# Operations of the first eighteen head pairs issued in another order

## The chip, the cores and the metric

The kernel runs on one core of a Trainium2 chip. The core has TensorE (PE: matmuls, with weight loads shown apart as PEld), VectorE (DVE), ScalarE (ACT), GpSimd (POOL), and SyncE (SP), which here only issues DMAs. Each engine works through its own queue strictly in the order in which the program gave it the instructions; engines wait for one another through semaphores. The metric is the device time of one execution in microseconds (us), median over runs.

## The reference

Two operators in a row, float32 in and out. Cosine attention over 8 batches, 12 heads, 448 positions and a head width of 64, then a feed-forward block with the activation h * relu6(h + 3) / 6 on the 3584 x 768 result.

```
q_n = q / (norm(q) + 1e-6);  k_n = k / (norm(k) + 1e-6)
scores = q_n @ k_n.T / tau            # tau = 0.1
attn = softmax(scores)                # 448 x 448 for each batch and head
x = (attn @ v), heads side by side    # 3584 x 768
h = x @ w_in                          # 768 x 2048
out = (h * clip(h + 3, 0, 6) / 6) @ w_out   # 2048 x 768
```

## The kernel before

The heads of a batch are taken two at a time, so there are 48 pairs, six to a batch. One load brings the queries, or the keys, of two pairs: an item (448 KB); items 2d and 2d+1 hold the queries and keys of pairs 2d and 2d+1 (up to item 13; from 14 on keys come first). An item is loaded (LQ), squared (SQ), summed along the head width (RE), made into a reciprocal norm (NO: logarithm and exponent on ACT, the last two of four steps on DVE where the name ends in v), scaled and cast to bf16 (NM), and transposed on PE into a PSUM bank (TR; from item 14 on by a DMA, XD). Copies CQ, CK and CS take the transposed queries and keys out of the bank. LV and VC load and cast the values.

For a pair, SC makes the scores in four groups (0 to 3; group 3 holds the last 64 keys of both heads), EX is the exponential on ACT, VA multiplies by the values on PE, FI divides by the row sums on DVE, and BK and CX (or the DMAs XP and XB) bring the result, transposed, into the block's input `xT`. A number behind the name is the item or pair, then the group; a letter is the engine: a for ACT, v for DVE, p for POOL. SQ.5.a.4.3 is the square of item 5 on ACT, three of its seven parts from part 4.

The block's first matmul takes units U of six matmuls each (one 128-wide slice of the 2048, all 448 rows of one batch); UA (relu on ACT) and UV (product on DVE) empty its PSUM bank. A batch's units need all six of its pairs, so the first U needs CX.0 to CX.5. The weights come by twelve DMAs W that POOL issues in its own queue: the first eight bring `w_in` in quarters of two DMAs (U 1 to 4 of a batch need the first two, 5 to 8 the next two, 9 to 12 the next, 13 to 16 the last), the other four `w_out`. W casts from float32 to bf16 on the way. From the 31st U on a unit is one of sixteen matmuls of the second product.

DP.n puts n filler matmuls on zeros into PE's queue (`busy_pv`, line 935 before and 934 after; D.n is line 930), which have no reader and no result that is used.

The order of the first eighteen pairs is written out in `PLAN`, a list of such operations in program order; the lines of `PLAN` are run one after the other by `run`, and each operation appends its instructions to the queues of its engines. So an operation that stands earlier in `PLAN` stands earlier in each of its queues, and nothing else orders them but data and buffers. In the first six pairs the scores go to two double banks in turn (the last figure of SC.i.g.bank); after `OPEN` six single banks are used in a ring, in the order of program. Seven float32 buffers hold items, so item 8 can be loaded once item 1 is scaled, and so on. After `PLAN` a loop does pairs 18 to 47 in a fixed pattern that the change does not touch.

```
def load_qk(j, *heads):
    needs(("NM", raw_before(j)))
...
def mm1_unit(b, fc):
    needs(*(("CX", i) for i in range(b * HP, (b + 1) * HP)))
    assert len(weights) <= 10 - 2 * (4 * fc // FCN)
...
def next_weights():
    o, w = weights.pop(0)
    nc.gpsimd.dma_start(out=o, in_=w)
...
    for line in PLAN:
        run(line)
```

Of the kernel before, what the change touches and what calls it, by code (L numbers as in the profile page):

```python
# [1110 lines left out]
```

## Time and profile before

| | before |
|---|---|
| median of 3 runs | 406.54 us (403.97, 406.54, 407.21) |
| profiled execution | span 404.4 us, 9618 instructions; the page gives no time of that execution outside its span |
| busy, share of the span | PE 393.7 us (97%), DVE 288.7 (71%), ACT 276.7 (68%), POOL 236.7 (59%) |
| granted TensorE clock | 1.00 over the whole span |
| DMA | 63.75 MB, mean 158 GB/s |

The busy share of PE counts the filler matmuls as work, and counts overlapping matmuls once. In the views below, a row of the timeline reads: start, length of the (merged) row, engine, line, operation, tiles, how many, and in brackets the idle time of the engine before it with what ended it. A row of the windows reads: from, to, length, then the busy time and count of each engine, the granted clock, the DMA share and GB/s.

### The profile page before, as it was taken

To read this page: it belongs to the slowest core of one execution; us is meant where nothing else is said; L and a number is where in the kernel's file an instruction comes from. 1 tells how busy PE (TensorE), PEld (TensorE's weight loads), DVE (VectorE), ACT (ScalarE), POOL (GpSimd) and SP (SyncE) were. 2 spreads that over 40 slices of the span, in tenths; PEclk is the share of its full clock that TensorE was granted. 3 is DMA by queue.
4 is the path that set the end of the run, shared out by engine and by line. 5 is a ranking of instruction groups with operands and counts; after the bars stand their busy time and mean duration, and the time that the engine had idled before them with its cause. 6 is when DMAs were issued, how large, how long until landed. Compare 5 with 4: busy or idle time off the path is not lost.

```text
span 404.4 us, 9618 instructions
## 1 busy us (share of the span) xinstructions
PE 393.7 (97%) x3689; PEld 234.5 (58%) x3689; DVE 288.7 (71%) x512; ACT 276.7 (68%) x604; POOL 236.7 (59%) x232
## 2 busy tenths in 40 slices
PE   7798999999999999999999999999999999999996
PEld 5566656555665555655555556555565556555564
DVE  5898787878498777777857887587656666655663
ACT  4899989887377687687768768768758755225230
POOL 4799945862744997588486875876664600510070
PEclk9999999999999999999999999999999999999999
DMA  8899999999877748786779659986863523140134
GB/s 285 247 235 243 221 221 213 170 219 202 181 168 179 167 111 209 185 222 129 169 200 194 140 149 163 180 190 136 193 147 76 112 45 63 36 88 20 25 74 99
DMA packets 93166, 63.75 MB, mean 158 GB/s; under 512 B 56128, under 2 KB 93120, under 8 KB 93120
## 3 DMA queue, kind: packets, MB, share of 16 engines
q1 hardware_dynamic: 87408, 56.45, 61.1%
q0 software_dynamic: 5312, 6.29, 9.5%
q8 instruction: 29, 0.48, 0.6%
q10 hardware_dynamic: 400, 0.39, 0.3%
q14 instruction: 17, 0.14, 0.1%
HBM read 45.61 MB, written 11.01 MB: 140 GB/s over the span
## 4 chain that ended last, share of the span: by engine, by line
PE 88%; ACT 4%; DVE 3%; DMA 3%; SPq 1%; issue 0%; DVEq 0%; ACTq 0%
PE M L580 23%; PE M L753 16%; PE PV L475 11%; PE Y L580 6%; PE Z L580 6%; PE M L435 6%; PE Z L753 5%; PE Y L753 4%; PE M L833 3%; PE M L627 3%; ACT at L453 3%; DMA big<-in_q_dram 3%; PE Y L435 1%; PE Z L435 1%; PE Y L833 1%; PE Y L627 1%
## 5 line engine op out<-in xcount | busy, mean ns | idle before, releaser
L453 ACT ACTIVATE at<-M 128x448 bf16<-128x448 f32 x194 | 96.8, 564 | 23.2 <-PE M L435 20.7
L580 PEld LDWEIGHTS <-w_in_sb 128*128 128x128 bf16 x768 | 72.3, 98 | 63.1 <-issue 2.5
L580 PE MATMUL M<-xT,w_in_sb 128*128 128x448 bf16 x504 | 107.4, 352 | 0.1
L286 POOL TENSOR_TENSOR nrm<-big,r 128x896 bf16<-128x896 f32 (+1 forms) x47 | 78.1, 1665 | 14.8 <-issue 4.6
L229 POOL TENSOR_TENSOR big<-big 128x896 f32<-128x896 f32 (+5 forms) x45 | 68.1, 1519 | 14.8 <-DMA big<-in_k_dram 8.2
L589 ACT ACTIVATE u<-M,bias 128x448 bf16<-128x448 f32 x84 | 54.9, 655 | 26.3 <-PE M L580 26.0
L475 PEld LDWEIGHTS <-at 128*128 128x128 bf16 (+1 forms) x1536 | 54.1, 97 | 19.9 <-issue 12.1
L595 DVE SCALAR_TENSOR_TENSOR gT<-u,M 128x448 bf16<-128x448 bf16 x73 | 44.6, 617 | 29.2 <-ACT u L589 28.4
L475 PE MATMUL PV<-vx,at 128*128 128x65 bf16 (+1 forms) x1536 | 62.7, 194 | 0.0
L241 DVE TENSOR_REDUCE n<-big 128x14 f32<-128x896 f32 (+1 forms) x50 | 51.5, 1037 | 0.3 <-ACT big L227 0.2
L392 POOL COPY km<-tT 64x128 bf16<-64x128 bf16 x34 | 14.4, 424 | 61.9 <-PE M L435 25.9
L782 POOL TENSOR_TENSOR big<-big 128x384 f32<-128x384 f32 x11 | 11.8, 1077 | 54.6 <-ACT big L801 54.5
L753 PEld LDWEIGHTS <-gT 128*128 128x128 bf16 x288 | 27.8, 98 | 20.0 <-DVE gT L731 0.6
L753 PE MATMUL M<-w_out_sb,gT 128*128 128x384 bf16 x192 | 35.0, 326 | 0.1
L496 DVE TENSOR_TENSOR on<-PV,rc 128x512 bf16<-128x512 f32 x48 | 33.2, 691 | 1.7
L435 PE MATMUL M<-tT,kz 64*128 64x448 bf16 (+1 forms) x171 | 30.9, 351 | 0.5 <-ACT at L453 0.5
L453 ACT ACTIVATE at<-Y 128x448 bf16<-128x448 f32 x50 | 28.2, 564 | 4.3 <-PE Z L435 4.3
L753 PEld LDWEIGHTS <-gs 128*128 128x128 bf16 x224 | 21.5, 98 | 14.7 <-DVE gs L731 0.3
L453 ACT ACTIVATE at<-Z 128x448 bf16<-128x448 f32 x50 | 28.2, 565 | 2.6 <-PE M L435 2.6
L305 POOL CAST vx<-big 128x512 bf16<-128x512 f32 x39 | 28.2, 728 | 3.1 <-DMA big<-in_v_dram 3.0
L580 PE MATMUL Z<-xT,w_in_sb 128*128 128x448 bf16 x132 | 28.6, 353 | 0.0
L580 PE MATMUL Y<-xT,w_in_sb 128*128 128x448 bf16 x132 | 28.6, 352 | 0.0
(128 smaller groups left out, 574.7 us busy)
## 6 DMA issues: line engine op xcount, KB each, us to landing
big<-in_k_dram SPq DMA_DIRECT2D x24, 448.0 KB, 5.1
big<-in_q_dram SPq DMA_DIRECT2D x24, 448.0 KB, 4.5
out_dram<-o SPq DMA_DIRECT2D x107, 96.0 KB, 2.2
big<-in_v_dram SPq DMA_DIRECT2D x48, 128.0 KB, 4.7
big<-in_v_dram SPq DMA_DIRECT2D x48, 96.0 KB, 4.4
w_in_sb<-in_moe_w_in_dram POOLq DMA_DIRECT2D x8, 384.0 KB, 10.4
w_out_sb<-in_moe_w_out_dram POOLq DMA_DIRECT2D x4, 768.0 KB, 10.8
tT<-nrm SPq DMA_TRANSPOSE x34, 2.8
```

The costliest lines, as they stand in the source:

```text
L229: engines[e].tensor_tensor(out=o, in0=i, in1=i, op=ALU.mult)
L241: nc.vector.tensor_reduce(out=n2_and_r[0][:, d % 2, j % 2, c], in_=sq[:, :, :, :].rearrange("p g c d -> p (g c) d")[:, c, :], axis=AX.X, o ...
L286: engines[e].tensor_tensor(out=nrm[:, :, g, :].rearrange("p c g d -> p g c d"), in0=raw_of[j][:, g, :, :], in1=n2_and_r[4][:, d % 2, j % 2, :]
L305: (engines[e].copy if e == "a" else engines[e].tensor_copy)(out=o, in_=f)
L435: nc.tensor.matmul(o, ks, qt[rows], start=True, stop=True)
L453: nc.scalar.activation(out=o, in_=x, func=AF.Exp, scale=inv_tau)
L475: nc.tensor.matmul(pv_out(j, h), at[rows, n, q_cols(i // HP, j)], vt[rows, 3 + h if name == "M" else 5 * h + int(name[1]), :], start=(name ...
L496: nc.vector.tensor_tensor(out=on[:, :, :, :].rearrange("p j h d -> p h j d"), in0=pv4[:, :, :, 0:D], in1=rc[:, :, :].to_broadcast([128, 2, ...
L580: nc.tensor.matmul(ps[:, 0:S], w_in_sb[:, cc, fc * 128 : (fc + 1) * 128], x[:, cc, 0:S], start=(cc == 0), stop=(cc == CC - 1),)
L589: nc.scalar.activation(out=u[:, :], in_=ps[:, 0:S], func=AF.Relu, bias=half_bias, scale=1.0 / 6.0)
L595: nc.vector.scalar_tensor_tensor(out=g[:, fc, c0 : c0 + S], in0=u[:, :], scalar=1.0, in1=ps[:, 0:S], op0=ALU.min, op1=ALU.mult,)
L753: nc.tensor.matmul(m, lhs[:, c, :], rhs[:, c, c0 : c0 + width], start=(base is None and c == 0), stop=(c == KC - 1), skip_group_check=True,)
```

## The change

Only `PLAN` changes; it has one line less, so that every line of the kernel behind it has a number lower by one afterwards. The operations are nearly the same ones in another order, and some go to another engine. The number of U, SC, EX, VA, TR, BK, W and loads is the same.

- Item 0 (queries) is loaded and prepared ahead of item 1 (keys). Before, item 1 came first, and item 0's norm stood behind the square of item 3 on ACT.
- The norms: before, NO.1 (items 2 and 3) stands ahead of EX.0.0 on ACT, as four ACT operations; afterwards it stands behind EX.0.1, as two ACT operations with the rest on DVE (NO.1.v). NO.3.v becomes NO.3, NO.4 and NO.5 become NO.4.v and NO.5.v.
- Both value loads LV.0 and LV.1 now stand directly behind the first six item loads in SP's queue; item 8's load stood between them.
- Fillers: 87 and two wide ones before; 88 afterwards, of which 40 stand in one block ahead of the first transpose.
- The squares of items 10 to 13 and the scaling of item 10, which stood ahead of the first U on POOL, stand behind it. VC.0 to VC.3, all on DVE before, are split: VC.0 on DVE, VC.1 to VC.3 on POOL.
- W: before, the first W stands on POOL behind SQ.7.p and the second right behind it; afterwards both stand behind NM.6.p. The sixth stands behind NM.10.p, which itself needs NO.5.v; seven and eight stand behind VC.10.p, nine behind NM.12.p, ten to twelve behind NM.15.p.
- The first U stands ahead of SC.8.0 instead of behind it. The U are placed otherwise among pairs 8 to 17: all 30 first-product units now stand ahead of SC.13.3.

The diff, with the part up to the middle of the list in full:

```diff
 PLAN = [
-    "DP.1 LQ.1 DP.2 DP.1 DP.1 DP.1 DP.1 DP.1 SQ.1.a.0.4 SQ.1.a.7.4 DP.1 SQ.1.v.4.3 DP.1 SQ.1.p.11.3 LQ.0 DP.2 DP.3",
-    "LQ.3 DP.1 LQ.2 SQ.0.p.6.2 RE.1.0 RE.1.1 LQ.5 DP.2 SQ.0.a.0.6 SQ.0.p.8.6 DP.1 RE.0.0 RE.0.1 DP.1 NO.0.1 DP.1 DP.1",
-    "NM.1.v.1 DP.1 SQ.3.a.0.7 DP.1 LQ.4 DP.2 D.2 DP.1 DP.2 NM.1.v.0 LV.0 DP.1 DP.2 NO.0.0.v DP.4 SQ.2.a.0.7 TR.1.Y",
-    "CK.1.a DP.1 DP.1 DP.1 DP.2 RE.3 DP.1 RE.2 NM.0.p.1 CK.0.a SQ.5.a.4.3 DP.2 DP.1 DP.4 DP.1 LQ.8 NM.0.p.0",
-    "SQ.4.v.4.3 SQ.5.a.0.4 NO.1 DP.1 DP.2 SQ.4.p.0.4 LV.1 TR.0.Z DP.3 DP.1 DP.1 NM.3.p LQ.7 NM.2.p.0 CQ.0.v SC.0.0.0",
-    "RE.5 LQ.6 DP.1 DP.1 EX.0.0 SC.0.1.1 DP.1 RE.4 NM.2.v.1 EX.0.1 DP.1 DP.1 NO.2 NM.4.p DP.1 LQ.10 VC.0.v DP.1 DP.2",
-    "LQ.9 DP.1 SC.0.2.0 SC.0.3.1 TR.3.Y CQ.1.v VC.1.v LV.2 CK.2.v DP.2 DP.2 DP.1 DP.1 VC.2.v EX.0.2 SQ.7.p.0.7 LQ.11",
-    "W EX.0.3 TR.2.Z CQ.2.v SC.1.0.0 EX.1.0 SC.1.1.1 CQ.3.v DP.1 SC.1.2.0 TR.4.Z VC.3.v EX.1.1 EX.1.2 SC.1.3.1 VA.0.0",
-    "CQ.4.v EX.1.3 DP.1 CQ.5.v LV.4 DP.2 LV.3 SQ.6.a.0.7 NM.5.v.1 W DP.1 DP.1 RE.7 SC.2.0.0 RE.6 VA.0.1 NM.5.p.0",
-    "SC.2.1.1 VA.0.2 VA.0.3 SQ.8.p.0.7 EX.2.0 EX.2.1 DP.3 SQ.9.p.0.7 DP.1 SC.2.2.0 FI.0 CK.3.v TR.5.Z SC.2.3.1 EX.2.2",
-    "CK.4.v NO.3.v NM.6.p RE.8 VA.1.0 VA.1.1 SC.3.0.0 VA.1.2 VA.1.3 EX.2.3 SC.3.1.1 FI.1 EX.3.0 SC.3.2.0 EX.3.1",
-    "EX.3.2 SC.3.3.1 EX.3.3 VA.2.0 SQ.10.p.0.7 RE.9 SQ.11.p.0.7 W NM.7.p.0 VC.4.p CK.5.v DP.1 VA.2.1 VA.2.2 VA.2.3",
-    "FI.2 VC.5.p LQ.13 NO.4 SC.4.0.0 TR.6.Y SC.4.1.1 EX.4.0 CQ.6.v CQ.7.v VA.3.0 VA.3.1 RE.10 VA.3.2 NM.8.p SC.4.2.0",
-    "BK.2.Z EX.4.1 EX.4.2 VC.6.p VA.3.3 NM.9.p W W VC.7.p LQ.12 LV.5 SC.4.3.1 SC.5.0.0 CX.2.v NM.7.v.1 FI.3 EX.4.3",
-    "BK.0.Y CX.0.v SC.5.1.1 EX.5.0 EX.5.1 SC.5.2.0 BK.3.Y DP.1 RE.11 TR.7.Z CX.3.v VA.4.0 VA.4.1 SQ.13.p.0.7 CK.6.v",
-    "SC.5.3.1 EX.5.2 BK.1.Y NO.5 NM.10.p EX.5.3 OPEN VA.4.2 CK.7.v SQ.12.p.0.7 SC.6.0 DP.1 CS.7.v VA.4.3 EX.6.0",
-    "CX.1.v CS.6.v SC.6.1 SC.6.2 TR.8 SC.6.3 EX.6.1 W W LQ.15 FI.4 VA.5.0 BK.4.Y VA.5.1 VA.5.2 CQ.8.v CQ.9.v EX.6.2",
-    "VC.8.p CX.4.v SC.7.0 VA.5.3 VC.9.p FI.5 TR.9 SC.7.1 EX.6.3 EX.7.0 SC.7.2 SC.7.3 CK.8.v CS.9.v CK.9.v VA.6.0",
-    "VA.6.1 CS.8.v VA.6.2 VA.6.3 BK.5 CX.5.v EX.7.1 SC.8.0 LQ.17 EX.7.2 EX.7.3 U EX.8.0 NM.11.p SC.8.1 SC.8.2 FI.6",
-    "RE.13 UA LQ.18 U EX.8.1 EX.8.2 SQ.15.p.0.7 W UV SC.8.3 U LV.7 LQ.14 UA VA.7.0 RE.12 UA VA.7.1 EX.8.3 TR.10",
...
+    "LQ.0 LQ.1 SQ.0.a.0.6 SQ.0.a.6.2 RE.0.0 SQ.0.p.8.6 RE.0.1 SQ.1.a.0.4 SQ.1.p.4.3 RE.1.0 SQ.1.a.11.3 SQ.1.a.7.4",
+    "RE.1.1 LQ.3 NO.0.0 NM.0.v.1 NM.0.v.0 DP.4 DP.4 DP.4 DP.4 DP.4 DP.4 DP.4 DP.4 DP.4 DP.4 TR.0.Z LQ.2 NO.0.1",
+    "SQ.3.a.0.7 NM.1.v.1 NM.1.p.0 DP.3 TR.1.Y CQ.0.a RE.3 LQ.5 SQ.5.p.0.4 SQ.2.a.0.7 LQ.4 CK.0.v DP.4 DP.4 SC.0.0.0",
+    "SQ.5.a.4.3 RE.2 EX.0.0 LV.0 LV.1 CK.1.v RE.5 CQ.1.v SQ.4.v.4.3 SC.0.1.1 EX.0.1 NO.1.v DP.4 DP.2 SC.0.2.0 EX.0.2",
+    "DP.3 SC.0.3.1 LQ.6 SQ.4.p.0.4 RE.4 NM.3.p DP.4 DP.2 SC.1.0.0 VC.0.v EX.0.3 DP.1 SC.1.1.1 LQ.7 EX.1.0 DP.4",
+    "SC.1.2.0 DP.1 VA.0.0 TR.3.Y VC.1.p VA.0.1 NM.2.v.1 NO.2 LQ.8 NM.4.v LQ.10 EX.1.1 CK.2.v NM.2.p.0 DP.3 SC.1.3.1",
+    "CK.3.v DP.1 TR.2.Z CQ.2.v VA.0.2 VA.0.3 EX.1.2 EX.1.3 VC.2.p SQ.6.a.0.7 NM.5.p.1 NM.5.p.0 CQ.3.v FI.0 RE.6 DP.1",
+    "SC.2.0.0 SC.2.1.1 TR.4.Z CQ.5.v CQ.4.v DP.1 VA.1.0 EX.2.0 EX.2.1 SC.2.2.0 VA.1.1 VA.1.2 VA.1.3 FI.1 SC.2.3.1",
+    "EX.2.2 DP.2 SC.3.0.0 EX.2.3 EX.3.0 BK.0.Y SC.3.1.1 SQ.7.p.0.7 EX.3.1 RE.7 NO.3 VA.2.0 VA.2.1 CX.0.v VA.2.2",
+    "VA.2.3 FI.2 TR.5.Z BK.1.Y CX.1.v SC.3.2.0 SC.3.3.1 CK.5.v VC.3.p VA.3.0 CK.4.v EX.3.2 DP.4 SC.4.0.0 EX.3.3 DP.1",
+    "SC.4.1.1 EX.4.0 LQ.9 VA.3.1 SQ.8.p.0.7 RE.8 SQ.9.p.0.7 VA.3.2 RE.9 EX.4.1 DP.1 SC.4.2.0 EX.4.2 NM.7.v.0 BK.2.Z",
+    "CX.2.v LQ.11 NM.6.p LV.2 VA.3.3 TR.6.Y NM.7.v.1 FI.3 NO.4.v CQ.6.v SC.4.3.1 DP.1 SC.5.0.0 DP.1 TR.7.Z EX.4.3",
+    "SC.5.1.1 W W VC.4.p VA.4.0 CQ.7.v EX.5.0 W VA.4.1 SC.5.2.0 VA.4.2 CK.6.v CS.6.v BK.3.Y EX.5.1 SC.5.3.1 CK.7.v",
+    "CX.3.v CS.7.v EX.5.2 EX.5.3 NM.8.p VA.4.3 OPEN SC.6.0 VC.5.p FI.4 TR.8 CQ.8.v CQ.9.v W SC.6.1 EX.6.0 SC.6.2 LV.4",
+    "LV.3 NM.9.p EX.6.1 LV.5 VA.5.0 LQ.13 VA.5.1 BK.4.Y EX.6.2 VA.5.2 VA.5.3 SC.6.3 CX.4.v FI.5 SC.7.0 EX.6.3 SC.7.1",
+    "TR.9 EX.7.0 EX.7.1 BK.5 VC.6.p VA.6.0 VA.6.1 CX.5.v CK.8.v VA.6.2 VA.6.3 FI.6 SC.7.2 SC.7.3 CK.9.a W U EX.7.2",
+    "EX.7.3 UA CS.8.v CS.9.v SQ.11.p.0.7 RE.11 SC.8.0 SC.8.1 VC.7.p VA.7.0 EX.8.0 EX.8.1 VA.7.1 U UA VC.9.v",
+    "SQ.10.p.0.7 UV RE.10 VA.7.2 VA.7.3 FI.7 SC.8.2 SC.8.3 NO.5.v VC.8.p U UV VA.8.0 EX.8.2 EX.8.3 UA U VA.8.1 UA",
+    "VA.8.2 VA.8.3 SC.9.0 EX.9.0 SC.9.1 UV UV FI.8 U SC.9.2 EX.9.1 UA UV NM.11.p SC.9.3 TR.11 EX.9.2 EX.9.3 VA.9.0",
+    "CK.11.v U NM.10.p CK.10.a TR.10 CS.10.v VA.9.1 VA.9.2 CS.11.v VA.9.3 CQ.10.v SC.10.0 SC.10.1 W UA SQ.13.p.0.7 UV",
+    "RE.13 CQ.11.a VC.10.p BK.8.Y CX.8.v U LQ.12 SQ.12.v.0.7 EX.10.0 FI.9 SC.10.2 EX.10.1 U UA UV UA SC.10.3 EX.10.2",
+    "EX.10.3 RE.12 U UA UV UV LQ.15 U UA UV SQ.15.v.0.7 U UA SC.11.0 W W LQ.14 EX.11.0 SC.11.1 U VC.11.a SQ.14.p.0.7",
+    "NO.6 EX.11.1 VA.10.0 VA.10.1 UV RE.14 VA.10.2 VA.10.3 NM.12.p W U XP.6 SC.11.2 FI.10 UA UV UA BK.10 U RE.15",
+    "EX.11.2 SC.11.3 EX.11.3 UA NM.13.p UV LQ.16 SQ.16.p.6.1 UV VA.11.0 BK.9.Z CX.9.a NO.7 VA.11.1 VA.11.2 VA.11.3",
+    "CX.10.v U UA U FI.11 BK.11 CX.11.a U UA UA UV TR.13.Y CS.12.v CK.13.v LQ.18 CS.13.v TR.12 LQ.17 SQ.17.a.4.3",
+    "NM.14.p CK.12.v UV CQ.13.v LV.7 LV.6 U U XD.14 SQ.16.a.0.6 U UA UA U UV UA LQ.19 UV CQ.12.v VC.12.a SC.12.0 UV",
...
+    "WS.7.0 SQ.22.v.4.3 SC.17.2 VA.16.2 VA.16.3 U UA EX.17.2 U RE.21 NO.10 NM.20.p SC.17.3 FI.16 WS.y4.0 CK.19.v",
+    "CS.18.v VA.17.0 UV XP.14 GL.0 EX.17.3 XB.16 VC.18.p",
```

27 rows, old and new, of the table PLAN are left out of this document.

## The prediction

> **What bounds the kernel now.** I first cut the span at events in the timeline: the first exponential (14.90 us), the first on the six-bank ring (37.60), the first unit of the block's first product, U1 (43.90), and the loop's start (117.1). The windows of these stretches show a different limit in each (the rest is the loop).
>
> ```profile
> span 404.4 us, 9618 instructions
> core 0: us, PE busy (x) PEld busy (x) DVE busy (x) ACT busy (x) POOL busy (x), PEclk, DMA share, GB/s
> 0.00:14.90 14.90, 10.83 (x77) 8.18 (x78) 9.40 (x35) 8.30 (x21) 7.90 (x23) 1.00 0.83 260
> 14.90:37.60 22.70, 20.54 (x287) 13.54 (x287) 21.81 (x48) 21.64 (x39) 22.13 (x20) 1.00 1.10 256
> 37.60:43.90 6.30, 6.08 (x109) 4.32 (x110) 4.36 (x15) 6.24 (x14) 6.30 (x6) 1.00 1.20 215
> 43.90:117.10 73.20, 73.10 (x718) 42.40 (x716) 55.65 (x100) 56.84 (x128) 41.34 (x39) 1.00 1.01 199
> ```
>
> From 43.90 on PE has work without a break (73.10 of 73.20), and the loop is the same afterwards. So the change is worth what it moves U1, less what PE loses between U1 and the loop. Ahead of U1, PE's busy time is padded by fillers; from 14.90 to 37.60 ACT, DVE and POOL are all above 95%, and before 14.90 everyone waits for loads:
>
> ```profile
> 4.28 0.72 ACT L227 ACTIVATE big<-big 128x256 f32<-128x256 f32 x2 [2.26 <-DMA big<-in_k_dram]
> 5.49 0.52 ACT L227 ACTIVATE big<-big 128x384 f32<-128x384 f32 x1 [0.49 <-DMA big<-in_q_dram]
> 5.93 0.21 ACT L269 ACTIVATE ln<-n 128x14 f32<-128x14 f32 x1
> 6.76 0.21 ACT L276 ACTIVATE r<-le 128x14 f32<-128x14 f32 x1
> 8.60 0.95 ACT L227 ACTIVATE big<-big 128x896 f32<-128x896 f32 x1 [1.63 <-DMA big<-in_k_dram]
> 9.46 0.20 ACT L269 ACTIVATE ln<-n 128x14 f32<-128x14 f32 x1
> 11.88 1.04 ACT L227 ACTIVATE big<-big 128x384 f32<-128x384 f32 x2 [0.27 <-DMA big<-in_k_dram]
> 13.59 0.56 DVE L229 TENSOR_TENSOR big<-big 128x384 f32<-128x384 f32 x1 [1.27 <-DMA big<-in_q_dram]
> 14.90 0.92 ACT L453 ACTIVATE at<-SC 128x896 bf16<-128x896 f32 x1 [0.99 <-PE SC L435]
> ```
>
> Item 1 lands at 4.28, item 0 at 5.49, and items 3, 5, 4 by 8.60, 11.88, 13.59. Item 0's norm starts only at 9.46, as it stands behind the square of item 3; its copy into `tT` then stands on DVE behind the square of item 4, which waits until 13.59. That is how the first exponential comes to 14.90.
>
> **Part 1, up to the first exponential.** The loads are as large as before and go out in like order, so the arrivals stay: item 0 at 4.28, item 1 at 5.49.
>
> ```profile
> 4.75 1.15 DVE L241 TENSOR_REDUCE n<-big 128x7 f32<-128x448 f32 x2
> 7.29 1.15 DVE L286 TENSOR_TENSOR nrm<-big,r 128x448 bf16<-128x448 f32 x2
> 2.47 5.55 PE L935 MATMUL PV<-xT 128*128 128x248 bf16 x26 [2.47 <-DVE vx L988]
> 8.40 1.22 PE L935 MATMUL PV<-xT 128*128 128x248 bf16 x10
> ```
>
> Item 0's squares on ACT end by 5.0, item 1's three by 6.4; DVE's four half sums (0.58 each) run from 5.1 and end at 6.3 for item 0, 7.4 for item 1. Two norms of 1.04 (5.93 to 6.97 in the trace) end on ACT at 7.5 and 8.5, and item 0 is scaled on DVE by 8.7, item 1 by 9.5, half on DVE and half on POOL. The block of 40 fillers takes PE to 9.3 (26 take 5.4, at half the later pace, 14 more take 0.105 each by the second filler row). So item 0's transpose starts at 9.3, item 1's about 10.0. The copy of the keys stands on DVE behind the sum of item 3 and ends near 11.0; eight fillers and the scores bring group 0 to 11.6. But on ACT the first exponential now stands behind a part of the square of item 5, which lands at 11.88: 11.88 + 0.43 = 12.3. Gain 2.6. The bounds: 11.6 if item 5 comes early, 14.0 if it comes as late as the sixth item does now (13.59). I take 12.3, as five items stand in SP's queue up to it both times.
>
> **Part 2, from there to the ring (22.70 us).** The exponentials of six pairs are the same on ACT; what differs is the norms between them.
>
> ```profile
> 25.24 0.22 ACT L269 ACTIVATE ln<-n 128x28 f32<-128x28 f32 x1
> 25.62 3.50 ACT L453 ACTIVATE at<-SC 128x448 bf16<-128x448 f32 x5
> 35.57 0.24 ACT L269 ACTIVATE ln<-n 128x28 f32<-128x28 f32 x1
> 36.65 0.53 ACT L453 ACTIVATE at<-SC 128x448 bf16<-128x448 f32 x1
> 37.60 0.98 ACT L453 ACTIVATE at<-M 128x448 bf16<-128x448 f32 x2 [0.43 <-PE M L435]
> ```
>
> A four-step norm takes ACT 1.08 (35.57 to 36.65), a two-step one 0.38. Before, three of the first and one of the second kind lie here, afterwards two of each: 0.70 less. One wait comes in: VC.1 is now on POOL, ahead of the scaling of item 2, and needs all of LV.1.
>
> ```profile
> 9.74 5.02 SPq L212 DMA_DIRECT2D big<-in_v_dram  x4
> big<-in_v_dram SPq DMA_DIRECT2D x48, 96.0 KB, 4.4
> 20.03 1.68 POOL L229 TENSOR_TENSOR big<-big 128x896 f32<-128x896 f32 x1 [0.42 <-DMA big<-in_k_dram]
> 27.53 1.69 POOL L286 TENSOR_TENSOR nrm<-big,r 128x896 bf16<-128x896 f32 x1
> 23.18 0.95 POOL L286 TENSOR_TENSOR nrm<-big,r 128x448 bf16<-128x448 f32 x1
> 36.79 0.60 POOL L305 CAST vx<-big 128x512 bf16<-128x512 f32 x1
> ```
>
> LV.1 goes out in four parts, the last near 14 (9.74 + 5.02, less its own issue); I put its issue near 13.6 now, its landing 4.4 later, at 18.0. POOL comes to VC.1 at 17.3 (NO.1's reciprocals at 15.6 plus 1.7). Of the 0.7, half reaches ACT through item 2's transpose: 0.35 (bounds 0 and 1.0). So the first exponential on the ring comes at 12.3 + 22.7 - 0.7 + 0.35 = 34.65, against 37.60.
>
> **Part 3, to U1.** In the trace U1 comes 6.0 after that exponential without the score group SC.8.0, which now stands behind it (43.61 instead of 43.90).
>
> ```profile
> 43.29 0.38 PE L509 MATMUL M<-ident,on 128*128 128x128 bf16 x4 [0.16 <-DVE kz L354]
> 43.61 0.36 PE L435 MATMUL M<-tT,kz 64*128 64x448 bf16 x2
> 43.90 1.31 PE L580 MATMUL M<-xT,w_in_sb 128*128 128x448 bf16 x6
> ```
>
> The last back transpose (43.29) waited for key copies on DVE. These now stand behind FI.5 and CX.5, and one goes to ACT. What is then left is ACT, busy 6.24 of the 6.30 us with the exponentials of pairs 6 and 7, fourteen operations of one bank each. U1's bank is free after eleven of them (behind EX.7.1): 11/14 of 6.3 are 4.95, and 0.4 more because SC.6.3 stands on PE behind a back transpose whose bank the copies of pairs 8 and 9 must leave first. So the chain would allow U1 at 40.0. What is late next is the weights:
>
> ```profile
> 21.65 1.52 POOL L923 DMA_DIRECT2D w_in_sb<-in_moe_w_in_dram  x2
> L923 POOL DMA_DIRECT2D w_in_sb<-in_moe_w_in_dram x8: 662/695/855, 21.6 to 51.5; - x8
> DMA to landing us min/median/max: 8.0/10.4/13.0
> ```
>
> Before, the first two W go out at 21.65 and 22.5, so that even at 13.0 they lie ready 8 us before U1. Now POOL does ten more operations first: from 18.0, three casts of 0.57, three halves of 0.93, three squares of 1.64 and one scaling of 1.66 make 11.1, so the W go out at 29.1 and 29.8. With L for the landing time, U1 is at the later of 40.0 and 29.8 + L. The median, 10.4, gives 40.2: 3.4 earlier than 43.6.
>
> **Part 4, between U1 and the loop.** PE's instructions are the same apart from U1's place, so its 73.2 us stay if nothing new keeps it waiting.
>
> ```profile
> 58.43 1.31 PE L580 MATMUL Z<-xT,w_in_sb 128*128 128x448 bf16 x6
> 45.25 0.63 ACT L589 ACTIVATE u<-M,bias 128x448 bf16<-128x448 f32 x1 [0.27 <-PE M L580]
> 84.63 1.30 PE L580 MATMUL Y<-xT,w_in_sb 128*128 128x448 bf16 x6
> 85.77 1.30 PE L580 MATMUL Z<-xT,w_in_sb 128*128 128x448 bf16 x6
> ```
>
> U9 needs the sixth W. U9 comes 14.53 after U1 in the trace (43.90 to 58.43). Eight units of 1.14 (84.63 to 85.77) leave 5.4 for nine score groups, eight value groups and two transposes, 0.28 for each. The new order puts three score groups, four value groups and a back transpose more ahead of U9: 2.3, so U1 + 16.8 = 57.0. The sixth W stands on POOL behind items 11 and 10, whose norm stands on ACT behind the relu of U2. U2 ends at U1 + 3.4 (two units, four groups); the relu takes 0.6, the norm's two steps on ACT 0.4, its two on DVE, behind FI.7, about 0.9 (an estimate), two scalings 3.3: W6 at U1 + 8.6 = 48.8. PE then waits for L - 8.2. SP's queue has no item load between item 14's and a transpose that waits for FI.7, so W6 meets little traffic; I take L between the minimum and the median, 9.2: a wait of 1.0 (bounds 0 and 4.8). W8 goes out 3.6 after W6, U13 comes 5.8 after U9, so it costs nothing more. The last of `w_out` goes out near 78; the 31st unit is not before 93.
>
> The other engines stay below PE there. DVE's 55.65 us grow by some 5: two sums, two whole squares and two whole scalings more (1.1 each), two casts less; ACT's 56.84 by some 4: two casts, a whole square and the last exponentials of pair 7 more. Both stay under 62 of 73. If that cover went, the place would be pairs 14 to 17, where DVE also has the weight sums. The end of the list (XP.14, a copy of g) moves behind the last stores; its first reader is two units into the second loop turn, some 9 us on: nothing.
>
> **Sum.** -3.4 + 1.0 = -2.4 on the span: 404.4 to 402.0. The median of the runs, 406.54, lies 2.1 above the profiled span, and I carry that over: 404.1 us. The three runs lie 0.8% apart, so about 1% (4.1 us) is what a measurement tells from no change.
>
> [...]
>
> **Rivals.**
> A. The weights land in 8.0. Then U1 follows the chain at 40.0 and U9 finds W6: -3.6, 400.8 on the span, 402.9. For it: the minimum in the trace, and POOL's queue has W alone or in pairs as before. Against: the pair at 21.65 was followed by the busiest DMA windows (1.10, 1.20), and W1 and W2 fall into the same stretch.
> B. Slower: the weights are the bound. With one L for all, U1 = 29.8 + L gains 13.8 - L, and the wait at U9 takes L - 8.2, so the gain is 22.0 - 2L. It is nil at L = 11.0, and at 13.0, the longest in the trace, it is a loss of 4.0: 408.4, or 410.5. For it: ACT ties W6 to U2, so that a late first pair delays the later ones. Against: 11.0 is above the median. [...]
> C. The opening gains little: item 5 arrives with the sixth load's time, 13.6, and the first exponential is at 14.0. U1 is then at 41.7, W6 ties to it, and the gain is 1.9 - 1.0 = 0.9: 403.5, or 405.6. For it: SP now sends LV.1 behind LV.0 at once. Against: it goes out behind item 5.
>
> **How the numbers follow.** Chances: my forecast 0.42, A 0.22, B 0.20, C 0.16. The range reaches from a little past A, 401.3, to most of the way to B, 409.2. Faster by over 1% (below 402.5): half of A and a quarter of mine, 0.22. Slower by over 1% (above 410.6): half of B, and 0.05 for a late `w_out` that comes on top, 0.15. The rest, 0.63, is within 1%.
>
> **What would show it.** The first exponential at 12.3 and the first on the ring at 34.7; the first W at 29.1; U1 near 40.2, its idle ended by a DMA of `w_in_sb`; a gap ahead of U9 ended by the same; the last VA.17.0 near 114.6. A first exponential after 13.5, a U1 after 42, or PE gaps above 2 us between U1 and the loop would make the prediction wrong.

## The result and the profile after

The changed kernel takes 411.08 us (median; 409.85 to 411.93), beside it the kernel before 405.88: a ratio of 1.014 with a 95% interval of 1.0098 to 1.0182. It is slower, where 404.1 and no difference were forecast; 411.08 lies above the range. The time of an execution lies 1.7 to 2.0 us above its span (411.93 and 410.1, 406.21 and 404.3), so spans can be compared as times; those of one kernel often scatter by 2 to 3.5 us (401.9 to 405.4 for the kernel before in one series). A span of a single profile therefore shows where time lies, and the medians show how much there is.

The windows of the profile after, cut at the same events as before (first exponential, first on the ring, U1, the loop's start); the columns are from, to, length, then busy time and count of PE, PEld, DVE, ACT, POOL, clock, DMA share, GB/s:

```profile
core 0 of [0], span 410.1 us
0.00:12.14 12.14, 8.89 (x74) 6.79 (x75) 8.99 (x32) 7.32 (x18) 5.62 (x21) 1.00 0.87 271
12.14:40.49 28.35, 23.10 (x301) 14.40 (x299) 22.16 (x50) 21.63 (x39) 22.02 (x21) 0.94 0.80 199
40.49:45.59 5.10, 5.10 (x99) 3.67 (x100) 3.51 (x10) 4.97 (x12) 5.09 (x6) 1.00 1.17 245
45.59:120.46 74.87, 74.02 (x721) 42.43 (x719) 62.08 (x106) 61.26 (x136) 35.55 (x34) 1.00 0.95 201
```

The first stretch is 2.76 shorter than before, as forecast. The second is 5.65 longer. ACT, DVE and POOL have the busy time that they had (21.6, 22.2, 22.0; before 21.6, 21.8, 22.1), but in 28.35 instead of 22.70 us: they stand still for the difference. What they wait for is in PE's queue. The waits of PE from 14 to 45 us (the waiting line, engine and line waited for; us, times, longest):

```profile
PE PV L934 <- DVE on L495: 3.0, 3, 1.2
PE Z L331 <- POOL nrm L285: 1.0, 1, 1.0
```

The rows of PE's timeline with these:

```profile
20.24 0.56 PE L331 MATMUL Z<-ident,nrm 128*128 128x128 bf16 x7 [0.98 <-POOL nrm L285]
...
22.42 0.37 PE L934 MATMUL PV<-xT 128*128 128x248 bf16 x1 [1.13 <-DVE on L495]
22.72 0.93 PE L434 MATMUL SC<-tT,kz 64*128 64x448 bf16 x4
...
36.24 0.27 PE L934 MATMUL PV<-xT 128*128 128x248 bf16 x1 [1.19 <-DVE on L495]
```

L934 is a filler, L495 the division FI. A filler has no reader, but it writes into the bank `PV` that FI reads (columns 260 to 507, where FI reads 0 to 259). Where it stands close behind an FI in program order, it waits until FI is done on DVE (at 22.37 for FI.0), and the scores behind it on PE wait too. The kernel before has no such wait: where its fillers come, FI is done. The four score matmuls in the third row take 0.93 us at a granted clock of 0.50; the same four take 0.55 at 1.00 in experiment 10. The windows around them have the clock in the third column from the right:

```profile
18.80:22.25 3.45, 1.51 (x26) 1.06 (x25) 2.56 (x7) 1.89 (x3) 3.25 (x4) 1.00 0.95 326
22.25:25.66 3.41, 3.24 (x25) 1.68 (x25) 1.80 (x4) 1.73 (x2) 3.41 (x4) 0.50 0.92 294
```

After a stretch with PE busy for 1.51 of 3.45 us, the granted clock is half for 3.41 us. In the profile before, it was 1.00 up to 404 us.

The loop, whose instructions are the same, takes 289.6 us (120.46 to 410.1) instead of 287.2. PE has three waits at its start; before it had none there:

```profile
121.67 0.37 PE L434 MATMUL M<-tT,kz 64*128 64x448 bf16 x2 [0.67 <-DVE o L639]
...
132.90 0.35 PE L579 MATMUL Z<-xT,w_in_sb 128*128 128x448 bf16 x1 [0.77 <-DMA xT<-on]
...
143.66 1.46 PE L752 MATMUL M<-w_sum,gs 128*128 128x384 bf16 x8 [0.32 <-DVE big L809]
```

So the longer span has three parts: U1 2.0 late (45.59, against 43.61 for before without SC.8.0), 1.3 between U1 and the loop (PE stands idle for 0.85 there, against 0.10 before), 2.4 in the loop.

### The profile page after: what moved, and what is told of

Its sections match the earlier page's. It is cut to its first block, busy times and chain, and to the rows that moved or that the text cites. A ratio compares the mean times of both kernels' runs of the same rounds, so it can differ in the third digit from the quotient of the medians.

```text
span 410.1 us, 9621 instructions
## 1 busy us (share of the span) xinstructions
PE 395.0 (96%) x3688; PEld 233.3 (57%) x3688; DVE 294.8 (72%) x514; ACT 278.9 (68%) x606; POOL 229.7 (56%) x228
## 4 chain that ended last, share of the span: by engine, by line
PE 77%; DVE 7%; DMA 3%; issue 2%; POOL 2%; SPq 1%; ACT 1%; POOLq 0%; DVEq 0%; ACTq 0%
PE M L579 20%; PE M L752 14%; PE PV L474 9%; PE Y L579 7%; PE Z L579 6%; PE Z L752 5%; PE M L434 4%; PE Y L752 3%; PE M L832 3%; DMA w_in_sb<-in_moe_w_in_dram 2%; DVE n L240 1%; DVE on L495 1%; PE Z L434 1%; PE Y L434 1%; DMA xT<-on 1%
## 5 line engine op out<-in xcount | busy, mean ns | idle before, releaser
L452 ACT ACTIVATE at<-M 128x448 bf16<-128x448 f32 x200 | 99.5, 567 | 20.1 <-PE M L434 18.1
L579 PE MATMUL M<-xT,w_in_sb 128*128 128x448 bf16 x468 | 99.6, 352 | 0.4 <-DMA w_in_sb<-in_moe_w_in_dram 0.4
L285 POOL TENSOR_TENSOR nrm<-big,r 128x896 bf16<-128x896 f32 (+1 forms) x43 | 73.1, 1701 | 23.7 <-ACT r L275 12.8
L228 POOL TENSOR_TENSOR big<-big 128x896 f32<-128x896 f32 (+4 forms) x42 | 65.0, 1549 | 20.8 <-DVE n L240 8.3
L588 ACT ACTIVATE u<-M,bias 128x448 bf16<-128x448 f32 x78 | 51.1, 657 | 25.2 <-PE M L579 24.7
L594 DVE SCALAR_TENSOR_TENSOR gT<-u,M 128x448 bf16<-128x448 bf16 x67 | 40.8, 616 | 28.1 <-ACT u L588 27.7
L579 PE MATMUL Y<-xT,w_in_sb 128*128 128x448 bf16 x162 | 35.1, 352 | 0.0
L495 DVE TENSOR_TENSOR on<-PV,rc 128x512 bf16<-128x512 f32 x48 | 33.2, 691 | 1.9 <-DVE rc L494 0.2
L434 PE MATMUL M<-tT,kz 64*128 64x448 bf16 x176 | 31.3, 351 | 1.0 <-DVE o L639 0.7
L304 POOL CAST vx<-big 128x512 bf16<-128x512 f32 x42 | 31.0, 739 | 0.2
L452 ACT ACTIVATE at<-Y 128x448 bf16<-128x448 f32 x45 | 25.6, 569 | 4.3 <-PE Z L434 3.0
```

The source lines that it names most:

```text
L228: engines[e].tensor_tensor(out=o, in0=i, in1=i, op=ALU.mult)
L285: engines[e].tensor_tensor(out=nrm[:, :, g, :].rearrange("p c g d -> p g c d"), in0=raw_of[j][:, g, :, :], in1=n2_and_r[4][:, d % 2, j % 2, :]
L304: (engines[e].copy if e == "a" else engines[e].tensor_copy)(out=o, in_=f)
L434: nc.tensor.matmul(o, ks, qt[rows], start=True, stop=True)
L452: nc.scalar.activation(out=o, in_=x, func=AF.Exp, scale=inv_tau)
L495: nc.vector.tensor_tensor(out=on[:, :, :, :].rearrange("p j h d -> p h j d"), in0=pv4[:, :, :, 0:D], in1=rc[:, :, :].to_broadcast([128, 2, ...
```

## The experiments

Theory: the fillers behind FI, with the half clock that follows, are the main cause. Rivals: POOL and DVE hold item 2 up by working beside each other; the DMAs at the end of the list; DVE's or SP's order there. "List end" is the start of VA.17.0, and the loop starts 0.3 to 0.4 behind it; all times are us. Each ratio is to runs of the kernel before in the same series. The diffs show only those parts of `PLAN`'s lines that differ.

| | median | ratio to before | U1 | list end | span |
|---|---|---|---|---|---|
| before | 404.2 to 405.9 | | 43.90 | 116.80 | 404.4 |
| after | 411.08 | 1.0140 [1.0098, 1.0182] | 45.59 | 120.12 | 410.1 |
| 1 no filler behind FI | 406.96 | 1.0046 [1.0022, 1.0071] | 40.30 | 117.47 | 406.6 |
| 2 and more fillers ahead | 408.55 | 1.0085 [1.0051, 1.0118] | 40.48 | 116.81 | 406.4 |
| 3 XP.14 earlier | 410.89 | 1.0132 [1.0093, 1.0171] | 46.08 | 120.96 | 410.5 |
| 4 POOL and DVE apart | 411.71 | 1.0164 [1.0138, 1.0189] | 45.59 | 121.45 | 409.9 |
| 5 weights earlier | 408.86 | 1.0116 [1.0092, 1.0140] | 40.22 | 118.43 | 407.8 |
| 6 and DVE's end | 408.70 | 1.0112 [1.0089, 1.0135] | 40.20 | 117.27 | 406.2 |
| 7 one filler less | 407.86 | 1.0082 [1.0062, 1.0101] | 43.28 | 118.22 | 406.9 |
| 8 before, four fillers more | 412.96 | 1.0221 [1.0199, 1.0243] | 50.73 | 123.64 | 411.0 |
| 9 weights spread | 406.03 | 1.0035 [1.0014, 1.0055] | 40.21 | 114.33 | 404.3 |
| 10 after, nine fillers more | 409.60 | 1.0128 [1.0083, 1.0173] | 43.39 | 118.99 | 407.8 |
| 12 NM.20 on DVE | 405.80 | 1.0030 [1.0008, 1.0053] | 40.26 | 114.26 | 404.0 |
| 13 LV.9 earlier | 404.87 | 0.9995 [0.9976, 1.0014] | 40.79 | 114.80 | 403.0 |
| 14 two DVE operations moved | 403.42 | 0.9975 [0.9956, 0.9993] | 40.41 | 114.23 | 401.6 |

**1. The five fillers behind FI.0, FI.1 and FI.3 taken out.**

```diff
-CQ.3.v FI.0 RE.6 DP.1
+CQ.3.v FI.0 RE.6
-EX.2.2 DP.2 SC.3.0.0
+EX.2.2 SC.3.0.0
-SC.4.3.1 DP.1 SC.5.0.0 DP.1 TR.7.Z
+SC.4.3.1 SC.5.0.0 TR.7.Z
```

> The changed list without the five fillers that stand right behind the row divisions FI.0, FI.1 and FI.3. Theory 1 (a filler that follows FI in the list waits for FI on DVE and holds PE's queue, 3.0 us in three waits, and the idle PE then gets half its clock from 22.25 to 25.66): the first score of pair 2 comes at 21.3 instead of 22.7, the half clock goes or shrinks, U1 comes at 42 to 43 instead of 45.6, the span loses 2.5 to 3.5 of the 410.1 us. Rival 2 (POOL sets the pace: the half scaling of item 2 takes 1.77 us beside DVE's scalings instead of 0.95): pair 2 gains under 1 us and U1 stays after 44.5.

The first exponential on the ring comes at 34.74 and U1 at 40.30, 5.3 earlier than after and within 0.1 of the forecast 34.65 and 40.2. No half clock is granted up to 404 us; PE's busy time in the stretch that was thin is 2.88:

```profile
18.80:22.25 3.45, 2.88 (x46) 2.01 (x47) 2.56 (x6) 2.72 (x4) 3.25 (x5) 1.00 0.70 205
```

Two thirds of the loss are gone (1.0140 to 1.0046), but the kernel is not faster than before, though U1 is 3.3 earlier. What takes the lead back is in PE's waits from 40 to 121:

```profile
PE M L626 <- DMA w_out_sb<-in_moe_w_out_dram: 1.3, 1, 1.3
PE M L579 <- DMA w_in_sb<-in_moe_w_in_dram: 1.2, 1, 1.2
PE Z L434 <- DVE tT L353: 0.5, 1, 0.5
PE M L434 <- DVE o L639: 0.5, 1, 0.5
```

**2. Nine fillers more ahead of the transpose of item 2, on top of that.** `CK.3.v DP.1 TR.2.Z` becomes `CK.3.v DP.10 TR.2.Z`.

> As the run before, with nine more fillers ahead of the transpose of item 2, where PE has nothing else (from 19.2 to 20.2 us). If the half clock comes from PE's idle stretch between 18 and 22 us, it is gone here for certain, and U1 comes up to 1 us earlier than without these fillers where the half clock was still there, and at the same time where it had gone already. If the half clock has another cause, it stays in both.

U1 40.48, no half clock: nothing is gained, as the first experiment had none either (the median is 1.6 higher, but the intervals overlap).

**10. The nine fillers alone, the five behind FI kept.**

> The changed kernel with all its fillers kept and nine more ahead of the transpose of item 2, which fill PE's idle 0.98 us there (19.26 to 20.24); the waits behind FI.0, FI.1 and FI.3 stay. Theory: the half clock from 22.25 follows PE's thin stretch of 18.8 to 22.2, and the waits cost their time without it; with that stretch fuller no half clock is granted, the waits behind FI stay at about 3.0 us, and U1 comes 1 to 1.5 earlier than 45.59, near 44.3; span near 409. Rival: the wait behind FI.0 alone (1.13 us up to 22.42) is what brings the half clock; then it is granted again near 22, and U1 and the span stay within 0.5 of 45.59 and 410.1.

This parts the wait from the clock. The waits behind FI stay at 3.0:

```profile
PE PV L934 <- DVE on L495: 3.0, 3, 1.2
```

No half clock is granted, and the window that was thin is less so:

```profile
18.80:22.25 3.45, 2.32 (x36) 1.59 (x35) 2.50 (x6) 1.32 (x3) 3.19 (x5) 1.00 0.66 211
```

U1 is at 43.39, 2.9 behind the second experiment, which is the 3.0 of the waits. The changed kernel's 45.59 is another 2.2 later: 1.0 of it is there already at the first scores of pair 2 (22.72 against 21.72), ahead of any effect of the clock on them; the other 1.2 comes behind them, with the half clock. So in these profiles the waits cost 3.0 and the clock some 1.2. The theory held; U1 came earlier than its 44.3, by about that 1.0, which is the later landing of item loads in the profile after (POOL's square of item 4 waits for its load there until 13.77; in the first experiment it runs at 12.35).

The medians of this kernel and the changed one do not part the clock from the rest (1.0128 and 1.0140). The single executions do: the changed kernel and that of the third experiment have the same opening, and of their eight executions four show a mean granted clock of 0.994 to 0.996, as the profile after does, and take 411.6 us on average; the other four show 0.998 to 1.000 and take 410.2. So the half clock does not come in every execution, and without it the changed kernel is still slower than before. None of the ten executions of the first experiment is below 0.998.

**7. Only the filler behind FI.0 taken out.**

> The changed kernel with only the one filler behind FI.0 taken out; the four behind FI.1 and FI.3 stay. Theory: that first wait starts the half clock, since PE is then idle for 1.1 us more in the sparse stretch ahead of 22.25. Without it the score groups of pair 2 start near 20.4, no half clock is granted before 380, and U1 comes near 42.0, as the later four fillers still hold PE back by about 1.7; span near 408. Rival: the half clock comes from the whole stretch being thin in work (the transposes of item 2 wait for POOL near 19) and stays, within 2 us of 22; then U1 is above 44 and the span within 0.8 of 410.

No half clock either; from 18.80 to 22.25 PE was busy for 2.46 of the 3.45 us. Waits of 1.9 are left, U1 is at 43.28 (forecast 42.0, the rival's bound 44). With either remedy, one wait less or nine fillers more, the clock in the profile stays at 1.00 from 18.80 to 25.66 (one of the four executions of the tenth experiment, not the profiled one, shows a mean of 0.996).

**8. The kernel before, with a filler put behind each of FI.0 to FI.3.**

```diff
-FI.0 CK.3.v TR.5.Z
+FI.0 DP.1 CK.3.v TR.5.Z
```

> The kernel before with one filler of 248 columns put directly behind each of FI.0, FI.1, FI.2 and FI.3 in the list, so that it stands on PE ahead of the transpose, the score groups or the back transpose that follow. Theory: each filler waits for FI's multiplication on DVE, as it writes to the bank that FI reads; by the trace of before the four would begin at 25.07, 28.17, 30.50 and 33.89 instead of 24.26, 27.03, 29.42 and 33.06, 3.8 us in all, of which half reaches the exponentials: U1 2 us later than 43.90, no half clock (PE is fuller there), span near 406.4. Rival: PE waits there but its queue catches up, as ACT and DVE set the pace; then U1 is within 0.5 of 43.90 and the span within 0.8 of 404.4.

Four matmuls (0.27 us for a single one in the profile before, at 34.67) make the kernel before 2.2% slower. The waits are 6.6 and not 3.8, the longest 2.1. Behind two stretches with PE busy for 1.46 of 3.44 and 1.27 of 3.41 us the granted clock is 0.50, which was not expected. PE's wait, and the windows:

```profile
PE PV L935 <- DVE on L496: 6.6, 4, 2.1
```

```profile
25.70:29.14 3.44, 1.46 (x20) 0.75 (x18) 3.38 (x6) 1.81 (x3) 3.01 (x2) 1.00 1.20 246
29.14:35.97 6.83, 5.81 (x68) 3.97 (x67) 2.62 (x6) 3.73 (x9) 6.82 (x9) 0.50 1.10 251
35.97:39.38 3.41, 1.27 (x18) 0.83 (x17) 2.88 (x4) 1.96 (x3) 3.41 (x5) 1.00 0.87 239
39.38:42.79 3.41, 3.41 (x37) 2.43 (x34) 2.39 (x5) 2.39 (x5) 1.74 (x2) 0.50 1.00 146
```

U1 comes 6.8 late (50.73). That shows the cause by itself, in the other kernel: the waits, together with the half clock beside them.

**4. POOL's and DVE's work on items 2 and 4 put on one engine each (NM.4 to POOL, VC.2 and VC.3 to DVE), on the second experiment.**

> As the run with fewer waits and more fillers, but with the scaling of item 4 on POOL (as before the change) instead of DVE, and the casts of pairs 2 and 3 on DVE instead of POOL. Rival 2 (POOL slowed by DVE's scalings): the half scaling of item 2 takes 0.95 again, its transpose starts at 19.2 to 19.5 instead of 20.2, and U1 comes 0.7 to 1.5 us earlier than without this edit. Theory 1 alone: U1 within 0.5 us of the run without this edit.

This does not part theory and rival. POOL's half scaling of item 2 takes 0.93 and ends at 18.79 (1.77 and 19.34 in the second experiment), as the rival had it. But the transpose of item 2 starts at 19.52 (19.48 in the second), since in both kernels it stands behind the ten fillers of `DP.10`, which fill PE until then:

```profile
18.45 1.23 PE L934 MATMUL PV<-xT 128*128 128x248 bf16 x10
19.52 0.55 PE L331 MATMUL Z<-ident,nrm 128*128 128x128 bf16 x7
```

What the two engines' work beside each other costs at this transpose therefore stays open. PE's wait for POOL there bounds it: 0.98 in the changed kernel, 0.71 in the first experiment. The main cause it is not, as the first experiment has the same scaling of 1.77 and its U1 is 5.3 earlier. New waits of PE come with the edit, for the casts, and a half clock at 42.39, behind a stretch with PE busy for 1.35 of 3.41 us:

```profile
PE PV L474 <- POOL vx L304: 2.6, 1, 2.6
PE PV L474 <- DVE vx L302: 1.1, 1, 1.1
```

**3. XP.14 moved ahead of the last loads and stores, in the changed kernel.** From behind `VA.17.0 UV` to behind `LV.11 U UV`.

> The changed list with one operation moved: the back transposes of pairs 14 and 15 (XP.14) stand behind FI.15, as early as before, and no longer behind the last stores. Theory 1 for the loop (the transposes by DMA of pairs 14 to 17 are 5.7 us late and a unit of the first product waits for them): the wait for xT at 132.9 us (0.77) goes, U1 and the end of the list stay, the span falls by 0.7 to 1.2 us. Rival (the loop's loss is DVE's, which is late with the store of the 36th unit): the loop still takes 289.6 us.

The opening is the changed kernel's, with the half clock (from 23.34). XP.14 goes out 5.1 earlier (119.59) and the wait for back-transposed tiles falls from 0.77 to 0.24, but the loop falls only from 289.6 to 289.2, about what that wait gave back: a single transfer was not the limit.

**5. The weights earlier on POOL, on the first experiment.** W6 to W8 behind VC.8, W9 and W10 behind SQ.14, W11 and W12 behind NM.13.

> The changed kernel without its five fillers behind FI.0, FI.1 and FI.3 (as in the first experiment), and with the weight loads moved up in POOL's order: W6 to W8 from behind the scaling of item 10 to behind VC.8 (about 42.8 us instead of 49.7), W9 and W10 to behind the square of item 14 (about 60.8 instead of 67.3 and 75.7), W11 and W12 to behind the scaling of item 13 (about 69.8 instead of 76.5). Theory: the 4 us that the first experiment lost again between U1 and the loop are PE's idle time at U9 (1.7 us between 50 and 60) and at U31 (1.3 us between 90 and 100), which the weights end. Then both gaps go, U1 stays at 40.3, VA.17.0 comes near 114.5 instead of 117.5 and the span is near 403.6. Rival: the time goes to DVE and ACT, which have more work ahead of the loop in this order; then the gaps turn up a little further on, VA.17.0 stays within 1 us of 117.5 and the span within 0.8 of 406.6.

The first half holds: U9 is at 57.46 and no longer waits. The second half turns the wait into another. With the four `w_out` loads issued between 61 and 69, the loads of query items and the DMA transposes from 40 to 100 us take 13.1 and 12.6 us (median; 5.8 and 6.3 in the first experiment). The DMA issues from 40 to 100 us, with size and time to landing:

```profile
big<-in_q_dram SPq DMA_DIRECT2D x3, 448.0 KB, 13.1
...
tT<-nrm SPq DMA_TRANSPOSE x3, 12.6
```

POOL's timeline, where the squares of items 19 and 18 wait for a load:

```profile
86.12 3.46 POOL L228 TENSOR_TENSOR big<-big 128x384 f32<-128x384 f32 x3 [10.86 <-DMA big<-in_q_dram]
```

DVE's timeline behind it, and PE's wait for DVE:

```profile
87.98 1.09 DVE L240 TENSOR_REDUCE n<-big 128x14 f32<-128x896 f32 x1 [3.15 <-POOL big L228]
```

```profile
PE Y L579 <- DVE gT L594: 2.3, 1, 2.3
```

U31 comes at 96.82 instead of 94.24. Neither theory nor rival had this cause; a gap further on and a list end within 1 us of 117.5 (118.43) are what the rival forecast, for another reason.

**9. W6 to W10 as there, W11 and W12 only behind the DMA transposes of items 14 and 15, and the end of the list in another order.** W11 and W12 behind the first square of item 17 (75.2); XP.14 ahead of LV.11, GL.0 behind the store of U34, the last store ahead of WS.y4.0.

> The changed kernel without the five fillers behind FI.0, FI.1 and FI.3; W6 to W8 at about 42.7 us (behind VC.8) as in the fifth experiment, W9 and W10 at about 60.7, but W11 and W12 only behind the first square of item 17, about 77.5, after the tile transposes XD.14 and XD.15 have gone out; at the end of the list the last store ahead of WS.y4.0, GL.0 behind the store of U34, and XP.14 ahead of LV.11 in SP's queue. Theory: the 12.6 us of XD.15 in the fifth experiment (6.3 without) came from the four w_out loads in flight beside it; with two of them gone by then, it lands in 7 or less, PE has no wait above 0.6 between 50 and 120, U9 is at 57.4, U31 near 92.8, VA.17.0 near 114.8 and the span near 402.7, 0.4% below the kernel before. Rival: the four w_out loads are late or in the way wherever they stand, as the loads of items take the DMA engines up to 75; then a wait of 1.5 or more stays between 85 and 100, VA.17.0 is above 116.5 and the span not below 404.4.

With two of the loads moved, the DMA transposes of `nrm` from 40 to 100 us land in 3.6 us (median), and the slowest of the whole execution takes 5.3 (12.6 in the fifth experiment):

```profile
tT<-nrm SPq DMA_TRANSPOSE x4, 3.6
```

U31 is at 92.77 and the list ends at 114.33, 2.5 ahead of before. The theory on the weights holds. But the span is 404.3: the loop takes all of the lead, with PE idle for 1.9 us at its start.

**6. The same order of DVE's end on the fifth experiment** (without XP.14).

> The kernel of the run before it, and the end of the list in another order on DVE: the store of the last unit ahead of the weight sum WS.y4.0 instead of behind it and a key copy, and the copy GL.0 some 8 us earlier, behind the store of U34. Theory: what the changed kernel still loses around the loop's start (0.5 to 0.7 us of PE's wait for that store, then 0.2 to 0.8 for back-transposed tiles and 0.3 to 0.4 for a sum, none of which the kernel before has) comes from DVE being late there; then these waits are gone or below 0.3 in all and the span is 1.0 to 1.5 lower than without it, near 402.4. Rival: it comes from SP's order, in which XP.14 and XB.16 stand behind the last stores; then the first wait goes but the other two stay, and the span falls by 0.5 at most.

The wait for the last store is gone; three waits are left at the loop's start, 0.94 in all. The span is 1.6 lower, the medians are alike (408.86 and 408.70), so a gain is not shown.

**12. The scaling of item 20 taken from POOL to DVE and to the end of the list, on the ninth.**

> The kernel of the ninth experiment with the scaling of item 20 taken from POOL, ahead of the key copies of CS.18, to DVE and the very end of the list, where the kernel before has it. Theory: the ninth kernel lost its lead at the loop's start because that scaling (1.69 us and more) stands on POOL ahead of CS.18 and beside DVE's WS.y4.0 (2.38 us there, 0.95 in the first experiment). Then WS.y4.0 takes about 0.96, the waits of PE for km (0.32) and for the bank ahead of the second product (0.51) go, the idle time of PE in the loop falls from 1.9 to 1.1 or less, and the span falls by 0.8 to about 403.4. Rival: SP's queue sets it, as XB.16 goes out at 120.1 behind the V loads and the last stores in either order; then XB.16 stays above 119.8, the wait for back-transposed tiles grows, and the span stays within 0.4 of 404.2.

WS.y4.0 takes 0.95 instead of 2.38 and the waits for km go, as in the theory. But PE's idle time stays (1.8), its wait for back-transposed tiles grows to 1.1, and XB.16 goes out at the same time, as the rival had it. SP's timeline, with no gap ahead of it:

```profile
115.04 2.65 SPq L211 DMA_DIRECT2D big<-in_v_dram  x4
117.78 2.47 SPq L614 DMA_DIRECT2D out_dram<-o  x4
120.29 1.29 SPq L520 DMA_TRANSPOSE xT<-on  x1
```

**13. LV.9 moved up in SP's queue, from behind XD.16 to behind VC.13.**

```diff
-CS.14.v VC.13.p VA.13.0
+CS.14.v VC.13.p LV.9 VA.13.0
-VA.13.3 LV.9 FI.13
+VA.13.3 FI.13
```

> The kernel of the twelfth experiment with the four loads of LV.9 moved up in SP's queue, from behind the transpose XD.16 (92.2 us) to behind the cast VC.13 (about 87), where SP stands idle. Theory: SP's queue sets the loop's start, since it issues from 90.9 to 124 nearly without a break, some 0.6 us each, and XB.16 goes out at 120.3 and the transfer behind it at 123.5, though pair 16 is divided at 114.2. With four issues fewer in that stretch XD.17 goes out at about 96.9 instead of 98.4, XB.16 at 118.8 or earlier, PE's wait for back-transposed tiles falls from 1.1 to 0.3 or less and the span from 404.0 to about 403.0. Rival: the end of that queue waits for the last stores and DVE's sums; then XB.16 stays within 0.5 of 120.3 and the span within 0.4 of 404.0.

XB.16 goes out at 118.75, the wait for back-transposed tiles is gone, and one wait is left in the loop. SP's row and PE's:

```profile
118.75 1.28 SPq L520 DMA_TRANSPOSE xT<-on  x1
```

```profile
121.07 1.64 PE L752 MATMUL M<-w_out_sb,gT 128*128 128x384 bf16 x9 [0.69 <-DVE gT L594]
```

The ratio goes from 1.0030 to 0.9995, with intervals that overlap. SP's queue, with some 0.6 us for an issue (1.2 to 1.3 for a DMA transpose) and full from 91 to 124 us in the twelfth experiment, set the wait for back-transposed tiles; the wait that is left is DVE's.

**14. Two operations moved on DVE, on the thirteenth.** WS.y4.0 ahead of the last store, and CQ.10 ahead of CS.11.

> The kernel of the run before it, with two copies moved on DVE: WS.y4.0 ahead of the last store again, as DVE stands idle for 0.98 us ahead of that store now (113.9 to 114.9), and the query copy CQ.10 ahead of the key copy CS.11, for which PE waited 0.5 us at 53.9. Theory: both waits are DVE's order; the one of 0.69 at 121.1 and the one of 0.5 go, PE has no idle time above 0.2 from U1 on, and the span is 1.0 lower at like U1, 402.0; against the kernel before 0.25% faster. Rival: the sum stays at about 2.2 us beside POOL's work and DVE is late all the same; then a wait of 0.5 or more stays at 121 and the span within 0.5 of 403.0.

PE has no wait at all up to 160 us from U1 on, and its windows are full:

```profile
40.00:114.00 74.00, 73.93 (x712) 42.28 (x712) 62.91 (x108) 61.19 (x136) 36.85 (x35) 1.00 1.06 216
114.00:160.00 46.00, 46.00 (x449) 27.12 (x447) 36.47 (x60) 34.91 (x79) 36.55 (x35) 1.00 0.72 171
```

403.42 us, 0.9975 [0.9956, 0.9993]: a little faster than the kernel before, whose PE has no wait from U1 to 160 us either. The new order's opening is worth something, about a quarter of a per cent, once nothing behind it takes it back.

**11. The kernel before, profiled once more.**

> The kernel before, unchanged, for a second profile: its shown profile has a span of 404.4, while most of its executions have spans of 402.0 to 403.0. Theory: the difference lies ahead of U1, where loads and the weights' landing set the pace; then a profile with a span near 402.4 has U1 near 42 and the same 73 us from there to the loop and the same 287.5 in it. Rival: it lies in the loop, through a transfer that lands late; then U1 stays at 43.9 and the loop takes 285.5.

Span 403.0, time 404.83, U1 at 42.70, and then 287.1 for the loop, much as before (287.2). The profile that the prediction started from was one of the longer executions, by 1.2 ahead of U1; the theory held on where the difference lies.

## Why the prediction was wrong

- **Part 1 was right.** First exponential 12.3, measured 12.14, behind the square of item 5 (11.71, its load the last to come). The size is uncertain by about 1 us: the event comes at 13.05 in the third experiment, which has the same opening, and at 13.21 in the second profile of the kernel before.
- **Part 2 failed**, in "what differs is the norms between them". Its 22.35 us from the first exponential to the ring were 28.35. Without the five fillers they are 22.93 (11.81 to 34.74), the rest well inside the bound of 1.0 that stood beside VC.1. The missing term is a wait that the change adds: fillers were counted as busy time without a reader and not as writers of a bank. It measured 3.0, with some 1.2 for the half clock; the rest lies ahead of 22.7, where two item loads landed later in this execution and POOL came to items 3 and 2 about 1.0 later (the third and seventh have the same, most others not).
- **Part 3 was right by luck.** U1 came 5.1 behind the first exponential on the ring (5.55 forecast), and at 40.30 without the fillers, where 40.2 was forecast. But no wait for `w_in` ended at U1, in any run: the chain set it, the way rival A had it. The landing time L was taken as 10.4, and the first two W landed in 6.4 and 8.6 us in the first experiment, by 38.3 at the latest, ahead of U1. The weights' issue was forecast at 29.1 and 29.8; it was 28.88 and 29.73 without the fillers and 32.72 and 33.56 with them.
- **Part 4 was right on U9 and wrong on `w_out`.** W6 came 9.3 behind U1 (8.6 forecast), U9 17.8 behind it (17.8). The wait of 1.0 was 0.37, and 1.2 in the first experiment. In the first experiment U31 also waits 1.3 for `w_out`. Its last load goes out at 77.2 and U31 comes at 94.2, as forecast (78, and not before 93), so it is the landing that was taken too short, and the wait that was put at nothing: these four loads take 14.1 us (median) and up to 20.4, where the prediction had 13.0 as its longest.
- **"Its first reader is two units into the second loop turn ... nothing" failed by up to 2.4.** The step looked at XP.14 and the copy alone, one operation at a time. What counts is SP's queue, which has 0.6 us for each issue and no gap there, and DVE's order ahead of the last store. The prediction named the place (pairs 14 to 17, where DVE also has the weight sums) but gave it no price.
- **Rivals.** B, the slower side, named the weights; they were late by more than 0.4 us only with some of the waits behind FI removed. C did not come about. None had the wait that decided it. Of the signs named, U1 after 42 was the one that spoke against the forecast.
- **The base.** The forecast of 404.1 started from a span of 404.4, which lies 1 to 2 us above the usual one (medians of 402.4 to 403.0 in the later series), and carried over 2.1 from span to time, where single executions show 1.7 to 2.0.

In the profile after, a filler that writes other columns than FI reads waits 1.13 and 1.19 us for it: the program keeps the two apart by bank and not by address. Whether the chip needs that wait, no run here shows.

## What to carry to other kernels

An instruction that was put in only to keep PE busy was ordered here like any other, by the bank it writes (3.0 us in three waits in the changed kernel, 6.6 in four in the eighth experiment): put it where that bank is free, never next behind an open reader. (No run here gave the fillers a bank of their own.) When an opening gets shorter, ask at each later meeting point (weights, stores, the queue that issues the transfers) whether it was on time by itself or by waiting for the opening; here three of them took back the whole lead of 3.3 us (2.1 against the second profile of the kernel before). Moving transfers earlier moves them beside other transfers (in the fifth experiment the DMA transposes then took 12.6 us instead of 6.3): look at what else is in flight.
